# Block products for a third batch, denominators from added tiles, and plain float32 scores

## The chip, the cores and the metric

The kernel runs on one core of one Trainium2 chip. The metric is device time in microseconds (us) of one execution, as the median of several runs. TensorE multiplies matrices into PSUM; VectorE, ScalarE and GpSimd work on SBUF and (but for GpSimd) PSUM; SyncE only issues DMAs.

## What is computed

The reference is attention for 4 batches of 12 heads (448 positions, head size 64) with a tanh cap on the scores, followed by two matrix products with a squared ReLU between them:

```python
scores = scale * np.matmul(q, k.transpose(0, 1, 3, 2))
scores = cap * np.tanh(scores / cap)
attn = np.exp(scores - np.max(scores, axis=-1, keepdims=True))
attn = attn / (np.sum(attn, axis=-1, keepdims=True) + 1e-09)
attn_out = np.matmul(attn, v)
x = attn_out.transpose(0, 2, 1, 3).reshape(B * S, H * D)   # 1792 x 768
r = np.maximum(x @ w_in, 0.0)                               # w_in 768 x 2048
out = (s * (r * r) + b) @ w_out                             # w_out 2048 x 768
```

The two weight matrices arrive as float64 and are turned into float32 bit by bit on the chip.

## The kernel before

**Attention.** Two heads make a pair, so a batch has 6 pairs. `load` fetches a pair's keys and queries (`kq`) and values. It also splits `kq` into a rounded part and a remainder, both float32r, in the tile `kh`: one copy (`kq_hi`, L371 to L376) and one subtraction (`kq_lo`, L377). `scores` computes one chunk of 128 keys against all 448 queries. For each of the two heads it multiplies three times (high by high, high by low, low by high), so a chunk is six float32r matmuls on 64 rows (L396). The last 64 keys of two pairs share one chunk, the tail, which has always used the unsplit float32 `kq` (L404). ScalarE then takes tanh (L408) and exp (L412) of each chunk. `pv` multiplies the chunks with the values in float32, four 32-column tiles side by side (L460, label `value`), and sums the same chunks with columns of ones for the denominators (`total`, L468): two calls of four float32 matmuls for each pair. A list `ADDED` can send a batch another way: the three full chunks are first added elementwise into the tile `acc` (label `add`), and one call of four matmuls sums that tile and the tail. Before, `ADDED` is empty.

**Products.** Values go through the two products as pairs of float16 tiles, high and low, with three matmuls for each product. `m1` is the first product, in steps of 9 matmuls with 448 columns (L706 to L708). The second has two forms. `m2` (L942 to L944) multiplies all of `w_out`: 24 steps of 12 matmuls with 448 columns for a batch. `m2pair` (L854, label `m2p`) works with seven half-width block products instead of eight: 42 steps of 12 matmuls with 224 columns for a batch. That form wants more from the other engines: sums and differences of the squared values (`less`, L805), their split (`e_hi`, `e_lo`), and mixed weights `ws` made once by `mix(p)` for each of three pairs of output blocks (`mcopy`, `mfull`, `msums`, `m_hi`, `m_lo`, L745 to L782), saved to HBM (`savem`) and loaded again (`load2`). Batches in `FAST` take it; before, these are 2 and 3.

**Order.** The program's operations are recorded by `Plan` and issued by hand: `ORDER` lists every operation by number, with a letter where ScalarE, VectorE or GpSimd can each do it (a, d, p). Each engine runs its part of that list in order. `SLOTS` says how many buffers each pool has; for example `ps_v`, the PSUM tile of `value` and `total`, has one.

Of the kernel before, what the change touches and what calls it, by code (L numbers as in the profile page):

```python
# [21 lines left out]
class Plan:  # L22
# [87 lines left out]
FAST = (2, 3)  # L110
ADDED = ()
# [3 lines left out]
    "w": 7, "kq": 3, "vp": 3, "ph": 5, "pt": 2, "rd": 3, "pw": 3, "num": 9, "cmp": 3, "x": 6, "r": 4, "sq": 5, "cs": 2,  # L115
    "kh": 2, "acc": 2, "ps_s": 2, "ps_v": 1, "ps_m": 2,
}
ORDER = """
9 10d 11d 0 921 13 20 4 17 5 21 922 923 14d 853 15d 915 22 854 855 26 18 924d 909 50 916 3 925 917 910 918d 859
27 12 911 23 19 856d 912d 926d 51 33 24 28 47 74 919 25 29 53 920a 865 48 52 913 999 34 30 78 16 977 54 31 860 6  # L120
# [12 lines left out]
247 295 1051 323 269 951 249 199 272 270 945 175d 298 324 46 326 329 952p 1052d 138 250 1055 946p 248 1062 251
273d 8 350 1056 947 252 305 201 276 309 277 942a 200 953 351d 304 325 306 301 330 274 355a 1057 367 352d 202d
327 111 307 275 328 176 954a 1058p 364 308 310 203 368 948a 278 876 1020 204 1059 279 358 311a 1063 357 331 280
313 205 955 435 206 332 365 281 1060a 336 333 359 207a 209a 1053 1064p 282 1027 956 334 361 356d 391 1065 211d
1054a 210 362 312 957 208 212 958 337 335 392 1066a 283p 394 388 1067 363 1476 431 395 1068 253 353 360 366 213a
1069 217d 338d 432p 448 1070 1071d 1072 254 963d 374 255 315 1095 433d 370 369 959a 371 389 215a 372 218 216 960
393 1073a 1074 214 390 375 373 1021 1075a 449 434 1077 445 1494 907d 964 1028 961a 342 1477 905d 436a 314 1495
446 256d 1029 1096 437d 442 439 1030a 376a 1097 401 397 443 396 1478 903a 440 398 1022 1033 1 1496 341 908 1031  # L140
316 339 496 1076 1032a 1023 1034 317 441 377 1089 399 450 318 402 319 400 1035 962 1036d 906 1024d 1497 472 475
1025 497a 320 1524 1525 1037 904 1090 498d 1078 1083 1026a 321d 1079 1488 447 1091 1038a 1526 1039 1489 1040
1041 476 403a 444 513 455 1098p 473 340 503 451 1084 1080a 1490 378 1085 1042 1099 452 404 514 1043a 1100 1086a
1491 1092d 642 438 380 453 1093 1094 1479 454 456 343 379 1081 1082 381 1045a 504 469 382 1087 1088 344 1482
1480a 1483 1492a 477 1493p 1518 505 1044 1527 1528a 474 1484 1101d 1108 257 470 1046 1109 510 1110 1047a 561 471
1113a 1115a 383 384 407 385 507 1519 501d 345 386d 1529d 457a 506 459 1560 478 482 1117p 284 387 1102d 1123p
1116 1111d 346 347 1498a 1125a 1103d 511 508 1118 460 483 479 480 1520 1048 481 406 502d 534 537 1561 1199 562a
1121a 348p 1124 1530 1126 405 1187 535 1181 499 538 1481d 1200 515 484a 1201 565 1122 1531 1188 1112 1189 1119d
2 1120 408 1182 409 1183 1202a 1114 1104d 1184d 1193 1185 1203 1499d 1521 512 540 1194 1195 1196d 578 461 1190a
509 516 563d 520 458 1562 1197 517 518 1204 521 519 1522p 1532 566a 1191 1198 1523p 567p 711 1105p 1563 541 579  # L150
536 1500 1501 1502 1503 1192 1186 572 569 410 1212 1213 1214 1227a 1564a 1485 1554 1205d 1504p 412 1106 411 539
1229a 413d 1565p 1533 1107 1555 1534a 1512 322 1206p 1513 1556 414 349 1228 646 1470 522a 1535p 1223p 1225a
1486p 1514 1505d 415 1471 573 570 1472 1473 580 1207d 488 485 487 486 489 1230 523 1217d 524 525 416 526 574
1219a 1226 1474a 1215d 1487d 543 542 527 571 547 602 575 1224 1557 1506 1221p 417 1507 1220 1218 1515 1508 462
1222 1536 1475p 463 1509 1516d 1558d 1216 1517d 1208d 1510a 710 1291 1292 1548 1549 1550 1293 1285 1286 1537
1294p 576 219 1287 490 1288d 1295 1566 1538 1511d 1303 1551 1567 1542 1539 1231 1127 1570 1209p 643a 1543 1552d
1584 1289 1544 1545 1540p 1297 544 545 546 548 599 1290 1128 1541d 528 1304 424a 1305 1546a 1210 603 1306d 1309d
1307 644d 1559p 1298 1553p 1299 1568 1296 1300p 1301 1308 464 1302 1211 1316 600 1317 1547p 1569 1310d 601 465
1318 1598 1327d 418a 1329a 1330 1331a 1333a 1311d 1332 605 491 492 493 494p 1334 659 647d 1328 529 1323a 530
549a 428a 466 426d 1580 1319d 1581 429 1324 1232 660 1571a 577 1321p 531 1582 564 1325a 585 581 648d 582 1312d  # L160
419 1326 583 584 586 1239 1240 1241 430 1242a 1233 1320 1322 1243 653 1245 1234 1244 1246 553 1251 604 1235 606
650 1247 532d 1336 551 1236a 651 587a 1248d 552 654 1252 707 645 655 1253 1594 1583 1237 1254d 1255 1335 1238
1595 1249 1256 568 1250 1313p 1264 1585a 591 1257d 467d 607 1265 1596 1266 1314 1279a 550 1147 1258d 1597 1591
1280 683 1275d 656 1259d 1271a 608 1315 609 1281d 1277d 1282 652 1273a 612 1148 1149 1274 1269d 1135 772 1150a
657 1267p 590 589 588 610 613 708d 611 680 1151 1278 1276 1270 1136 1129 1272 1599d 592 684 420d 724 658 614a
618 616 554 662 1152 661 681 555 556 663 709d 666 1141 1586 593 1268 594 427 422a 1137 725 1130 1131 423 664
1138a 1142 1143 1144d 1139 1132a 667 665 776 686 557 1260d 718 1133 1145 595 1146 685 726 719 1284 649 615 1134
1153p 596 682 1587 687 1588 1140 495 688 712a 558 617 1589 1160 1261p 597p 1161 1337 1162 1154d 1590 668a 559d
# [52 lines left out]
def attention_moe_kernel(  # L221
# [14 lines left out]
    D = 64  # L236
# [839 lines left out]
```

## Time and profile before

| | us |
|---|---|
| median of 3 runs (636.55 to 637.71) | 637.59 |
| the profiled execution | 638.84 |
| its span on the core | 637.1 |
| TensorE busy | 619.6 (97%) |
| VectorE busy | 420.9 (66%) |
| ScalarE busy | 355.3 (56%) |
| GpSimd busy | 143.7 (23%) |

In the views, PE is TensorE, PEld its weight loads, DVE VectorE, ACT ScalarE, POOL GpSimd, SP SyncE, and L12 is line 12 of the kernel. A float32 matmul shows as two records, a float16 or float32r matmul as one. The end of a matmul is modelled and lies past the start of the next, so the distance between starts tells what a matmul costs.

### The profile page before, as it was taken

The numbers are of one execution on the slowest core, as the hardware profiler recorded it, in microseconds if no ns is written. First come the engines' busy times: TensorE is split into PE (matmuls) and PEld (weight loads), VectorE is DVE, ScalarE is ACT, GpSimd is POOL, SyncE is SP. The second block draws the span as 40 slices with busy tenths as digits, with TensorE's granted clock in tenths as the row PEclk, the third lists the DMA queues.
The fourth block names the chain that finished last, engine by engine and source line by source line (L and its number), as shares of the span: only waits on it lengthen the run. The fifth ranks groups of instructions, "written<-read, shape, count | busy, mean of one in ns | idle before, by whom it ended". The sixth has DMA issues, their size and how long they took to land.

```text
span 637.1 us, 11673 instructions
## 1 busy us (share of the span) xinstructions
PE 619.6 (97%) x4548; PEld 343.7 (54%) x4548; DVE 420.9 (66%) x898; ACT 355.3 (56%) x490; POOL 143.7 (23%) x180
## 2 busy tenths in 40 slices
PE   5998999999999999999999999999999999999997
PEld 2333334444445444545445555555558996556997
DVE  6999789997978989798374472427674342355312
ACT  6999989998784756675455352234463101354100
POOL 0101131113453201412040233002253000246000
PEclk9998989999999999999999999999999999999999
DMA  7884654643335373653452324425166751500763
GB/s 291 289 252 135 198 166 154 212 141 127 111 94 163 119 272 130 222 186 105 144 180 100 123 106 151 162 99 195 34 228 256 232 180 46 215 1 1 227 221 117
DMA packets 51318, 101.68 MB, mean 160 GB/s; under 512 B 15808, under 2 KB 28224, under 8 KB 51264
## 3 DMA queue, kind: packets, MB, share of 16 engines
q1 hardware_dynamic: 51264, 100.95, 47.3%
q8 instruction: 35, 0.57, 0.4%
q14 instruction: 19, 0.16, 0.1%
HBM read 82.58 MB, written 18.17 MB: 158 GB/s over the span
## 4 chain that ended last, share of the span: by engine, by line
PE 76%; DVE 11%; DMA 9%; SPq 2%; issue 1%; POOL 0%; ACT 0%; POOLq 0%; ACTq 0%
PE ps_m L854 9%; PE ps_v L460 7%; PE ps_s L854 6%; PE ps_s L707 6%; PE ps_s L708 6%; PE ps_s L706 6%; PE ps_m L706 5%; PE ps_m L707 5%; PE ps_m L708 5%; PE ps_m L942 4%; PE ps_m L943 4%; PE ps_m L944 4%; PE ps_s L396 4%; PE ps_v L468 4%; DMA bed<-in_w_out 3%; DMA zd<-bed 2%
## 5 line engine op out<-in xcount | busy, mean ns | idle before, releaser
L854 PEld LDWEIGHTS <-bed 128*128 128x128 f16 x1008 | 96.5, 98 | 0.9
L408 ACT ACTIVATE bed<-ps_s,arena 128x896 f32<-128x896 f32 x84 | 83.1, 1009 | 23.9 <-PE ps_v L460 9.4
L328 POOL TENSOR_TENSOR bed<-bed 128x224 f32<-128x224 f32 (+5 forms) x51 | 53.6, 1059 | 170.0 <-ACT bed L798 91.2
L327 DVE TENSOR_TENSOR bed<-bed 128x224 f32<-128x224 f32 (+5 forms) x95 | 66.7, 721 | 36.0 <-DMA bed<-zd 15.4
L460 PE MATMUL ps_v<-bed 128*32 128x448 f32 x768 | 85.7, 552 | 3.1 <-DMA bed<-in_v 2.4
L412 ACT ACTIVATE bed<-bed,par 128x896 f32<-128x896 f32 x84 | 85.2, 1044 | 0.2
L707 PE MATMUL ps_m<-bed,w 128*128 128x448 f16 x192 | 67.9, 353 | 0.0
L707 PE MATMUL ps_s<-bed,w 128*128 128x448 f16 x192 | 67.8, 353 | 0.0
L706 PE MATMUL ps_m<-bed,w 128*128 128x448 f16 x192 | 67.5, 352 | 0.3 <-DVE arena L661 0.3
L942 PE MATMUL ps_m<-gt,bed 128*128 128x448 f16 x192 | 67.7, 352 | 0.0
L944 PE MATMUL ps_m<-gt,bed 128*128 128x448 f16 x192 | 67.7, 352 | 0.0
L943 PE MATMUL ps_m<-gt,bed 128*128 128x448 f16 x192 | 67.7, 352 | 0.0
L706 PE MATMUL ps_s<-bed,w 128*128 128x448 f16 x192 | 67.4, 351 | 0.0
L708 PE MATMUL ps_m<-bed,w 128*128 128x448 f16 x192 | 67.2, 350 | 0.0
L708 PE MATMUL ps_s<-bed,w 128*128 128x448 f16 x192 | 67.2, 350 | 0.0
L396 PE MATMUL ps_s<-kh 64*128 64x448 f32 x432 | 58.6, 393 | 6.2 <-DVE kh L373 4.6
L706 PEld LDWEIGHTS <-w 128*128 128x128 f16 x384 | 36.8, 96 | 39.3 <-issue 4.7
L396 PEld LDWEIGHTS ps_s<-kh 64*128 64x128 f32 x432 | 37.9, 189 | 37.2 <-issue 9.3
L794 ACT ACTIVATE bed<-ps_s,arena 128x448 f32<-128x448 f32 x32 | 20.2, 631 | 66.3 <-PE ps_s L708 57.5
L708 PEld LDWEIGHTS <-w 128*128 128x128 f16 x384 | 37.8, 98 | 35.4
L707 PEld LDWEIGHTS <-w 128*128 128x128 f16 x384 | 37.0, 96 | 34.4 <-issue 0.6
L460 PEld LDWEIGHTS ps_v<-bed 128*32 128x32 f32 x768 | 22.7, 111 | 48.9 <-issue 41.9
(126 smaller groups left out, 966.9 us busy)
## 6 DMA issues: line engine op xcount, KB each, us to landing
bed<-w SPq DMA_DIRECT2D x36, 512.0 KB, 4.2
bed<-in_w_out SPq DMA_DIRECT2D x24, 512.0 KB, 4.1
bed<-ws SPq DMA_DIRECT2D x24, 512.0 KB, 4.9
bed<-in_kq SPq DMA_DIRECT2D x24, 448.0 KB, 4.7
bed<-in_w_in SPq DMA_DIRECT2D x18, 512.0 KB, 5.6
bed<-in_v SPq DMA_DIRECT2D x24, 256.0 KB, 4.2
w<-bed SPq DMA_DIRECT2D x12, 512.0 KB, 5.0
ws<-bed SPq DMA_DIRECT2D x12, 512.0 KB, 4.3
```

Of the source, the lines that this page charges most:

```text
L327: "DVE": lambda: nc.vector.tensor_tensor(dst(), a(), c(), op),
L396: nc.tensor.matmul(P[kp][:, h, 0:S], a[:, kz, 0, c * 128:(c + 1) * 128], a[:, qz, 1], start=i == 0, stop=i == 2,)
L408: ("tanh", bb, c2, c), lambda: nc.scalar.activation(P[ke], P[kp][:, :, 0:S], AF.Tanh, scale=tsc[:, 0:1]),
L412: ("exp", bb, c2, c), lambda: nc.scalar.activation(P[ke], P[ke], AF.Exp, scale=par[:, 0:1]), r=["par"], w=[ke],
L460: nc.tensor.matmul(P[kp][o, 0, 0:S], P[kv][:, c, o], prob(c, h), start=(c == 0), stop=(c == NC))
L706: nc.tensor.matmul(ps[:, 0:S], wh, x[:, 0], start=(c == 0), stop=False)
L707: nc.tensor.matmul(ps[:, 0:S], wh, x[:, 1], start=False, stop=False)
L708: nc.tensor.matmul(ps[:, 0:S], wl, x[:, 0], start=False, stop=(c == NP - 1))
L854: nc.tensor.matmul(at(), w(g, zw), b(g, zb), start=g == 0 and x == 0, stop=g == n - 1 and x == 2,)
L942: nc.tensor.matmul(ps[:, 0:S], wh, ghi[:, f], start=(f == 0), stop=False)
L943: nc.tensor.matmul(ps[:, 0:S], wh, glo[:, f], start=False, stop=False)
L944: nc.tensor.matmul(ps[:, 0:S], wl, ghi[:, f], start=False, stop=(f == NF - 1))
```

## The change

`FAST` becomes batches 1, 2 and 3, `ADDED` becomes batches 1, 2 and 3, and a new list `SPLIT` leaves the float32r split of keys and queries to batch 3. Batches 0 to 2 compute their full chunks as `plain`: one float32 matmul for each head from the unsplit `kq`. The pool `kh` shrinks from two tiles to one, `acc` has one tile, `w` grows to eight. The DMA of `cap` is issued from ScalarE's queue. `ORDER` is new throughout.

```diff
-FAST = (2, 3)
-ADDED = ()
+FAST = (1, 2, 3)
+ADDED = (1, 2, 3)
+SPLIT = (3,)
 SLOTS = {
-    "w": 7, ...
-    "kh": 2, "acc": 2, "ps_s": 2, "ps_v": 1, "ps_m": 2,
+    "w": 8, ...
+    "kh": 1, "acc": 1, "ps_s": 2, "ps_v": 1, "ps_m": 2,
...
     def load(bb, c2):
...
-        kx = buf(("kh", bb, c2), "kh")
...
+        if bb in SPLIT:
+            kx = buf(("kh", bb, c2), "kh")
...
+        def plain():
+            for h in range(2):
+                a = P[("kq", bb, c2)][h * D:(h + 1) * D]
+                nc.tensor.matmul(P[kp][:, h, 0:S], a[:, 0, c * 128:(c + 1) * 128], a[:, 1], start=True, stop=True)
...
+        if last:
+            pe(("tail", bb, c2, c), rest, r=pair, w=[kp])
+        elif bb in SPLIT:
+            pe(("score", bb, c2, c), mm, r=[(kx, 0), (kx, 1)], w=[kp])
+        else:
+            pe(("plain", bb, c2, c), plain, r=pair[0:1], w=[kp])
...
+        queue = nc.sync if i else nc.scalar
```

The operations that change in number, from the lists of both kernels:

| operation | before | now |
|---|---|---|
| `score` (6 float32r matmuls) | 72 | 18 |
| `plain` (2 float32 matmuls) | 0 | 54 |
| `total` (4 float32 matmuls) | 48 | 30 |
| `m2` steps / `m2p` steps | 48 / 84 | 24 / 126 |
| `kq_hi` on VectorE, ScalarE, GpSimd | 10, 12, 2 | 0, 6, 0 |
| `kq_lo` on VectorE, GpSimd | 23, 1 | 5, 1 |
| `add` on VectorE, GpSimd | 0, 0 | 34, 2 |
| `less` on VectorE, GpSimd | 37, 27 | 55, 41 |
| `e_lo` on VectorE, GpSimd | 9, 7 | 20, 4 |
| `plus` on VectorE | 48 | 72 |

The first instructions on VectorE, before (`kh` is the split tile, `par` and `arena` hold constants, L540 and L545 unpack float64 weights):

```order
L373 CAST kh_64<-bed 128x896
L327 TENSOR_TENSOR kh_64<-bed,kh_64 128x896
L975 RECIPROCAL arena<-par 128x1
L976 TENSOR_SCALAR arena<-arena 128x1
L540 TENSOR_SCALAR bed<-bed 128x512
L545 SCALAR_TENSOR_TENSOR bed<-bed 128x512
L373 CAST kh_65<-bed 128x896
```

and now:

```order
L991 RECIPROCAL arena<-par 128x1
L992 TENSOR_SCALAR arena<-arena 128x1
L556 TENSOR_SCALAR bed<-bed 128x512
L561 SCALAR_TENSOR_TENSOR bed<-bed 128x512
L325 TENSOR_SCALAR bed<-bed 128x512
L567 SCALAR_TENSOR_TENSOR bed<-bed 128x512
```

The casts and subtractions for the first scores are gone, and the unpacking of weights stands first.

TensorE around the denominators of a pair of batch 1, before (L460 `value`, L468 `total`, L396 `score`):

```order
L460 MATMUL ps_v_68<-bed 32x448 x4
L468 MATMUL ps_v_68<-bed,ones 32x448 x4
L460 MATMUL ps_v_68<-bed 32x448 x4
L396 MATMUL ps_s_66<-kh_65 128x448 x6
L460 MATMUL ps_v_68<-bed 32x448 x4
L468 MATMUL ps_v_68<-bed,ones 32x448
L468 MATMUL ps_v_68<-bed,half 32x448
```

and now (L476 `value`, L484 `total`, L409 `plain`):

```order
L476 MATMUL ps_v_67<-bed 32x448 x8
L409 MATMUL ps_s_65<-bed 128x448 x2
L409 MATMUL ps_s_66<-bed 128x448 x2
L476 MATMUL ps_v_67<-bed 32x448 x4
L484 MATMUL ps_v_67<-bed,ones 32x448
L484 MATMUL ps_v_67<-bed,half 32x448
```

The first of the two `total` calls is gone, and each score is two matmuls in place of six.

VectorE now, on the way into batch 1's second product (L772, L781 to L784 and the 128x8x128 rows are `mix(1)`; rows of 128x224 are `less`, of 128x672 `e_lo`, on `gt` `g_lo`; L901 adds a block product):

```order
L772 SCALAR_TENSOR_TENSOR bed<-bed,arena 128x1024 x2
L781 TENSOR_TENSOR bed<-bed 128x4x128
L782 TENSOR_TENSOR bed<-bed 128x4x128
L783 TENSOR_TENSOR bed<-bed 128x4x128
L784 TENSOR_TENSOR bed<-bed 128x4x128
L332 TENSOR_TENSOR bed<-bed 128x224
L332 TENSOR_TENSOR gt<-bed,gt 128x448
L332 TENSOR_TENSOR bed<-bed 128x224
L332 TENSOR_TENSOR bed<-bed 128x8x128 x2
```

Before, the two mixes of the first pair of blocks stood among plain steps of batch 1, and nothing of batch 1 read what they made.

## Rows read from the trace of the kernel before

**Rows 1.** The page: busy time, share of the span, instructions of an engine.

```profile
PE 619.6 (97%) x4548; PEld 343.7 (54%) x4548; DVE 420.9 (66%) x898; ACT 355.3 (56%) x490; POOL 143.7 (23%) x180
```

**Rows 2.** Windows: stretch, length, busy time (count) of PE, PEld, DVE, ACT, POOL, granted clock, DMA.

```profile
0.00:20.00 20.00, 13.62 (x92) 5.58 (x92) 13.64 (x28) 12.74 (x15) 1.34 (x11) 1.00 0.84 314
20.00:60.00 40.00, 36.21 (x363) 14.99 (x363) 38.90 (x90) 40.00 (x50) 5.24 (x10) 1.00 0.68 217
60.00:100.00 40.00, 37.83 (x329) 14.54 (x325) 34.43 (x91) 35.73 (x42) 8.44 (x13) 0.91 0.53 162
100.00:140.00 40.00, 40.00 (x349) 17.86 (x341) 38.02 (x90) 39.99 (x56) 7.48 (x9) 1.00 0.59 195
140.00:180.00 40.00, 39.30 (x280) 19.01 (x277) 34.51 (x75) 32.42 (x49) 16.40 (x14) 1.00 0.36 113
180.00:220.00 40.00, 40.00 (x247) 19.41 (x246) 33.27 (x78) 25.09 (x40) 15.52 (x20) 1.00 0.36 114
220.00:260.00 40.00, 39.31 (x297) 17.77 (x296) 33.57 (x78) 27.60 (x35) 2.77 (x6) 1.00 0.62 211
260.00:300.00 40.00, 39.54 (x282) 19.55 (x280) 36.62 (x84) 25.50 (x34) 14.51 (x20) 1.00 0.47 157
```

**Rows 3.** Waits of PE: waiter, releaser, us in total, times, longest.

```profile
PE ps_s L396 <- DVE kh L373: 4.6, 1, 4.6
PE ps_v L460 <- DMA bed<-in_v: 2.4, 2, 1.4
```

**Rows 4.** Timeline of PE from 99.6: start, duration, line, operands, count.

```profile
99.96 1.69 PE L460 MATMUL ps_v<-bed 128*32 128x448 f32 x16
101.58 1.48 PE L396 MATMUL ps_s<-kh 64*128 64x448 f32 x12
102.99 0.18 PE L362 MATMUL ps_m<-brief,ones 128*128 128x1 bf16 x1
...
106.47 0.35 PE L706 MATMUL ps_m<-bed,w 128*128 128x448 f16 x1
...
108.18 0.17 PE L362 MATMUL ps_m<-brief,ones 128*128 128x1 bf16 x1
108.28 0.98 PE L404 MATMUL ps_s<-bed 64*64 64x448 f32 x8
109.19 0.96 PE L468 MATMUL ps_v<-bed,ones 128*32 128x448 f32 x8
109.96 2.44 PE L460 MATMUL ps_v<-bed 128*32 128x448 f32 x24
```

**Rows 5.** Timeline of PE in a second product of each form.

```profile
392.06 0.35 PE L943 MATMUL ps_m<-gt,bed 128*128 128x448 f16 x1
...
394.33 0.35 PE L943 MATMUL ps_m<-gt,bed 128*128 128x448 f16 x1
...
601.40 1.31 PE L854 MATMUL ps_m<-gt,bed 128*128 128x224 f16 x12
602.55 1.31 PE L854 MATMUL ps_m<-bed 128*128 128x224 f16 x12
```

**Rows 6.** Groups of DVE by line and shape: busy us, mean ns, idle before.

```profile
L551 DVE SCALAR_TENSOR_TENSOR bed<-bed 128x512 int32<-128x512 int32 x42 | 32.0, 772 | 1.2 <-POOL bed L321 0.6 <-ACT bed L319 0.4
L327 DVE TENSOR_TENSOR kh<-bed,kh 128x896 fp32r<-128x896 f32 x23 | 25.0, 1087 | 0.1
L338 DVE SCALAR_TENSOR_TENSOR bed<-bed,arena 128x256 f16<-128x256 f32 x48 | 24.6, 531 | 3.5 <-ACT bed L319 2.9 <-POOL bed L321 0.6
L327 DVE TENSOR_TENSOR bed<-bed 128x224 f32<-128x224 f32 x37 | 19.9, 556 | 13.8 <-ACT bed L798 7.5 <-POOL bed L328 6.0
L327 DVE TENSOR_TENSOR bed<-bed 128x672 f16<-128x672 f32 x9 | 8.6, 954 | 1.3 <-ACT bed L319 1.2
```

**Rows 7.** The page's DMA issues: size, median us from issue to landing.

```profile
bed<-ws SPq DMA_DIRECT2D x24, 512.0 KB, 4.9
ws<-bed SPq DMA_DIRECT2D x12, 512.0 KB, 4.3
```

More of the change, by code (lines that the diff above doesn't have):

```diff
@@ L114 @@
 SLOTS = {
[L115 to L116 removed]
+    "w": 8, "kq": 3, "vp": 3, "ph": 5, "pt": 2, "rd": 3, "pw": 3, "num": 9, "cmp": 3, "x": 6, "r": 4, "sq": 5, "cs": 2,
+    "kh": 1, "acc": 1, "ps_s": 2, "ps_v": 1, "ps_m": 2,
 }
 ORDER = """
[L119 to L120 removed]
@@ new lines @@
+856 917d 959 107 104 105 861d 976 90 38 86 87 131 862 915a 91 62 108 106 109 863 88 89 916 960 39 92a 135 136
+144 145 60 40 869 988 989 990d 957 113 961 208 864 918 857d 858 94 146 962d 865 963 977 991 61 93 112 96 95 978d
+141 866d 117 870 142 114 165 41d 867 137 97 132 138 115 116 871 98 118 59 875 166 143 63 168 139 931 119d 64
+872p 876 167 171 147 140 873 877 914 99 878d 148 981 120 121 65 879 982 932 169 149 964a 170 100 101 983 933
+859d 151 874a 152 134 212 868a 880a 881 172 123 122 150 958a 979 213 173 965 102p 966 984d 934p 124 215 967 218
@@ new lines @@
+326 267 1065 323 204 371 417 1056 1058 205a 202 206 299 1009 422 1004 269d 426 1506 427 941a 300 425 942 945d
+885a 1536 1537 1538 1507 324 997a 301 377 1005 1006a 357a 1452 337 946 382d 1010 1453 1016 1011 448 428 378 1071
+1059 1017 383d 2 327 358 361 360 1508 1012a 1018a 1454 1007 418 303 302 379 384 889d 1072 1013 419 1060 1019
+1020a 328 1014a 1008a 380 359 381 998 890 1073 1458 1509 887a 1021 476 304d 1074a 449 1459 1077 414 329 1455
+385a 450 362 1022 1023 433d 451 452 454 1456a 888 434d 387 330 429 1066 388 435 430 431 1078 1061 363 1024 455
@@ new lines @@
+516 1478 1172a 1184a 441 492 468 1496 547 493 1097a 1185 394 465 1086d 548 1087d 494 618 495 1166a 442 395p 1175
+1186 498 1500 1088 1511d 1501 466 574 1099p 1173 1100 1167 1474a 518 1176 1089 524d 1479 443 1177 543 542 499a
+500 1178d 619a 519 525d 1179 1502 1475p 520 575 503 521 1093a 1480a 522 1180 444 1168 1481p 270 445 544 501
+1095a 1497 1174 469 523 526 549 580 1482 1194 502 446d 470 576 550 1195 620d 1094 1483 1196 504 581 545 471 396
+1098 1187p 1188p 552 551 1484 1205a 527d 242 1464 1465 531 530 368 528 505 1209d 629 559d 1096 1503 553 560d
@@ new lines @@
+693 1545 1227 1235 1217 1218a 665 690a 1222 1236d 1237 1535d 1546p 1238 1223 670d 1523d 1224a 702 703 666 571
+667 1550 1564 671d 694 407 1225 1219 1214 599 1228 1239d 1229 1552 755 1547d 1220 704 1230a 598 1226 1565 650
+1231 691d 447 1551 651 572p 404a 1240p 1567a 1232 1246 1247 1248 668 672 1317 752 1259p 405 1261d 1260 695 1251a
+1252 1249a 1250 1257a 698 408a 669 1255a 692 1241d 727 724 1576 709p 673a 1253d 1263d 600d 701 728 1254 1256
+1129 1577 675 652 730 1117 725 769 676 729 674 753a 1242d 705 1264 1258 710d 711 731 726 706 707 411 1111 708
@@ L404, in rest @@
                     nc.tensor.matmul(P[kp][x * D:(x + 1) * D, h, 0:S], a[:, 0, c * 128:S], a[:, 1], start=True, stop=True)
-        pe(("tail" if last else "score", bb, c2, c), rest if last else mm, r=pair if last else [(kx, 0), (kx, 1)], w=[kp])
+        if last:
[4 more added lines that the diff above has]
+            pe(("plain", bb, c2, c), plain, r=pair[0:1], w=[kp])
         act(
@@ L992, in attention_moe_kernel @@
     for i, a in enumerate((cap, s, b)):
-        dma(("par", i), lambda i=i, a=a: nc.sync.dma_start(par[:, i:i + 1], a.to_broadcast([128, 1])), w=[("par", i)])
+        queue = nc.sync if i else nc.scalar
+        dma(
+            ("par", i), lambda i=i, a=a, queue=queue: queue.dma_start(par[:, i:i + 1], a.to_broadcast([128, 1])),
+            w=[("par", i)],
+        )
     gps(("units", -1), units, w=["one"])
```

186 lines of the change are left out of this document (86 added, 100 removed), and 8 rows, old and new, of the table ORDER.

## The prediction

> **What bounds the kernel now.** I read the page's first part, then the windows, then the waits and the timeline of TensorE. TensorE is busy 619.6 of 637.1 us [rows 1]. The windows show where it is not: 6.4 us are missing in the first 20, 3.8 from 20 to 60, 2.2 from 60 to 100, and from there under 1 us in any 40 us [rows 2]. The missing time belongs to the beginning, where VectorE is 97% and ScalarE 100% busy from 20 to 60. The longest single wait is the very first score's, 4.6 us for the first split of keys [rows 3]; the clock share of 0.91 from 60 to 100 is the other loss there [rows 2].
>
> Busy time hides small gaps, since ends are modelled. So I price TensorE by distances between starts. Two `value` chunks with the switch to another tile form take 101.58 - 99.96 = 1.62 us, so 0.75 a chunk and about 0.11 a switch; a `total` call is the same, 109.96 - 109.19 = 0.77; two scores take 1.41, 0.705 each; a tail takes 0.91 with a switch, 0.80 without; an `m1` step of nine 1.71 [rows 4]; an `m2` step of twelve 2.27, an `m2p` step 1.15 [rows 5]. Over the whole list: 128 x 1.71 + 48 x 2.27 + 84 x 1.15 + 144 x 0.75 + 72 x 0.705 + 12 x 0.80 = 593 us, some 106 switches at 0.1 make 10.6, and the small products for norms and biases 4.9, together 608. The span is 29 longer: 4.6 to the first matmul, about 3 for the last output, and some 21 of waiting, nearly all before 100 us. I call **lead** the time of a TensorE instruction less the TensorE work ahead of it. By the trace it grows to 21 us by 95 and stays near 23.5 from 190 on. So TensorE's own work and this lead are all that counts.
>
> **TensorE's work.** *Denominators:* batches 1 to 3 drop one `total` call for each of 18 pairs, 18 x 0.75 = 13.5 us less. *Second product of batch 1:* 24 steps of 2.27 (54.5) become 42 of 1.15 (48.3), 6.2 less. *Plain scores:* 54 of them. No row shows this form, so bounds: a plain score is two float32 matmuls, four records in two rounds, as in a `value` chunk, which streams the same 448 columns: 0.75 from below. The tail is the nearer relative (same operands, same 64 rows, weights of 64 columns instead of 128) and gives 0.80, or 0.91 if each carries a switch. I take 0.78, near the tail, since a score's 128-column loads cost it only about 0.05 for each round over 0.187 of streaming [rows 4]. That is 0.075 more than a split score, 54 x 0.075 = 4.1 more; ends +2.4 and +11. Fewer matmuls here is not less time.
>
> The Trainium skill (FP8 and Floating Point Precision, TensorE Precision Notes) counts four passes for true float32, against three for the split: it speaks against this edit, and the chunk of 0.75, four times the 0.19 of an `m1` matmul, agrees [rows 4]. The skill's Perfetto Trace Analysis (Engine Utilization) instead has float32 in its low and high form at half the output rate; by that a plain score would be 0.37 and the sum 22 us lower, and the chunk row disagrees.
>
> *Switches* rise from 106 to 111: 0.5 more. TensorE's sum is -13.5 - 6.2 + 4.1 + 0.5 = **-15.1 us**, 608 to 593.
>
> **The other engines.** The split disappears for three batches: VectorE loses 18 subtractions at 1.09 us and 10 casts, ScalarE 6 copies. This work stood in front of the first scores; the first score now needs only its load, and ScalarE's first tanh waits for `cap`, whose DMA leaves about half a microsecond sooner on ScalarE's queue and no longer stands in SyncE's. In return VectorE gets 34 additions over 896 columns (nearest row 1.09 each), 18 `less` at 0.56, 11 `e_lo` at 0.95 [rows 6] and 24 `plus`. All kinds together, VectorE's durations rise by some 41 us. Durations add up to 470 in the trace of before against 420.9 busy [rows 1], since neighbours overlap, so 0.895 of that: +36 us. ScalarE gains about 9.
>
> VectorE's place matters more than its sum. `mix` must now be ready for batch 1, some 100 us of TensorE work sooner than for batch 2. The tightest point is the second mixed pair of blocks: TensorE's third product there waits for the load of `ws`, that waits for its save, and that for the last `m_lo` of its first half. Ahead of that `m_lo`, by the new order and the rows of before, stand on VectorE: weight unpacking 101 us (rows like L551), `w_out` 73 (L338 and others), attention with 33 additions 72, `w_in` 42, `g_lo`, `less` and `e_lo` 41, `mix` 37, the rest 26: 392, times 0.895 = 350 us. TensorE's work ahead of its product is 358. Up to the same `m_lo`, VectorE's work before was 0.895 x 341 = 305 and nobody waited for it.
>
> The lead that this forces: VectorE starts at about 5.5 us, works 350 at some share s, then save and load take 4.3 + 4.9 [rows 7]. In stretches where much waits in its queue s was 0.97 (20 to 60), 0.95 (100 to 140), 0.92 (260 to 300); over 20 to 300 it was 249.3 of 280, 0.89, but much of that idle time was TensorE's doing [rows 2]. I take 0.955, between the two stretches in which both engines were full. Then the load lands at 5.5 + 366.5 + 9.2 = 381.2, and the lead is 381.2 - 358.4 = 22.8, against 23.5 before: **-0.7 us**. What the beginning gains (VectorE's queue ahead of a score was up to 13 us longer than TensorE's before, at most 4 now) is thus spent again by 380 us. After that point VectorE has 20 us and more in hand, and the end of the program is unchanged.
>
> Edits at nothing: the smaller `kh` and `acc` pools (the order already holds to them; if one tile is too few it shows as VectorE waiting for TensorE), and 18 more loads of 512 or 256 KB for batch 1: the same form's loads moved during batches 2 and 3 without a wait.
>
> **Sum.** From the profiled execution, 638.84 - 15.1 - 0.7 = 623.0. That execution lies 1.25 above the median of the runs, so **622** for a median.
>
> **The rivals.**
>
> *A, the forecast:* s from 0.935 to 0.97 gives leads from 29 to 17; with the ends of the plain score 615 to 630. Chance 0.63.
>
> *B, VectorE becomes the bound.* Place: the same `m_lo` and the additions on the way to it, each of which a `total`, and with the single `ps_v` the next pair's values, waits for. If s stays at the 0.89 of 20 to 300, the load lands at 408, the lead is 49.5, and the time 622 + 27 = 649. It decides at a lead of 38.6, s = 0.916: below that the kernel is slower than before. For it: VectorE reached 0.86 from 60 to 100 while TensorE waited [rows 2]. Against it: the queue that delayed TensorE there is now shorter. Chance 0.12 for slower, and 0.08 for the ground between A and the point of deciding, 630 to 638.
>
> *C, the beginning's gain stays.* With s at 0.97 or more and GpSimd taking its part, the lead falls to 14 to 16: 614, down to 611 with the cheapest plain score. For it: 20 to 60 did 0.97 with all engines full. Chance 0.12.
>
> *D, a plain score's two heads do not run side by side:* 54 x 0.75 = 40 more on TensorE, which then stands ahead of VectorE again: about 655. Against it: a split score's pair of heads does run side by side, six matmuls in 0.705 [rows 4]. Chance 0.02.
>
> *E, a plain score streams at half rate,* not a quarter: its 448 columns in two times the 0.19 of an `m1` matmul [rows 4], 0.38. That takes 54 x 0.40 = 22 us off TensorE's work, to 600 if TensorE alone sets the time; but all of it lies ahead of the tight point, where VectorE would keep most of it. Chance 0.03.
>
> **How the numbers follow.** A is likeliest: 622. The range takes in A, C and the ground between and leaves out most of B, D and E: 611 to 636. About 0.2% (1.3 us) is what a measurement can tell from no change. Faster: A, C, E and most of the ground between, 0.83; same, the rest of that ground, 0.03; slower, B and D, 0.14.
>
> **What would show it.** Right: plain scores 0.75 to 0.80 apart; `m2p` steps of batch 1 at 1.15; total matmul work near 593; TensorE's first matmul near 4 us; less idle TensorE before 100 us, and then some waits of TensorE between 100 and 380 for VectorE (`add`, `mix`) or for the loads of `ws`; VectorE's busy time near 457, its share up to 370 us about 0.95. Wrong: a plain score above 0.9; no waits after 100 us at all (C); or a lead above 30 at batch 1's `m2p` (B).

## The result, and the profile after

The changed kernel took 619.81 us (median of 4 runs, 618.26 to 620.61) where the kernel before, on the same chip, took 637.65 (636.55 to 638.56): a ratio of 0.972, 95% interval 0.969 to 0.975. The forecast was faster, 622, with a range of 611 to 636. The profiled execution took 619.09 us, with a span of 616.9, against 638.84 and 637.1 before. Experiments ran on several chips; each is compared by its ratio to the kernel before, timed on the same chip. The changed kernel, measured a second time beside the experiments, had 0.966 (0.964 to 0.969), so about 0.969 is its place on that scale, and 0.01 is 6.4 us.

The page of the changed kernel (answers to [rows 1]):

```profile
PE 603.0 (98%) x4512; PEld 347.6 (56%) x4512; DVE 450.7 (73%) x957; ACT 363.5 (59%) x509; POOL 158.1 (26%) x177
```

Its windows (columns as in [rows 2]: stretch, length, PE, PEld, DVE, ACT, POOL, granted clock, DMA):

```profile
0.00:20.00 20.00, 13.41 (x92) 4.37 (x92) 10.45 (x22) 13.17 (x15) 4.21 (x12) 1.00 0.85 327
20.00:60.00 40.00, 38.97 (x337) 12.50 (x338) 37.45 (x98) 39.16 (x47) 10.13 (x14) 1.00 0.63 208
60.00:100.00 40.00, 38.68 (x329) 12.84 (x325) 37.97 (x98) 38.34 (x46) 8.59 (x14) 1.00 0.64 194
100.00:140.00 40.00, 40.00 (x295) 16.07 (x291) 37.89 (x79) 39.21 (x55) 14.91 (x11) 1.00 0.58 177
140.00:180.00 40.00, 39.64 (x272) 16.16 (x264) 39.48 (x81) 37.34 (x55) 14.62 (x15) 1.00 0.34 100
260.00:300.00 40.00, 40.00 (x263) 19.49 (x262) 37.77 (x91) 20.82 (x31) 13.88 (x14) 1.00 0.47 151
340.00:380.00 40.00, 40.00 (x338) 29.36 (x335) 34.54 (x56) 25.07 (x39) 8.71 (x9) 1.00 0.63 224
```

Against [rows 2] TensorE gains 2.8 us of work from 20 to 60 and 0.9 from 60 to 100, and the clock share there is 1.00 in place of 0.91. VectorE is now 36 to 39.5 of 40 full all the way to 340, where before it had 33 to 35 from 140 to 260. ScalarE is full to 140. The waits of TensorE are short but for the first (waiter, releaser, us in total, times, longest; compare [rows 3]):

```profile
PE ps_s L409 <- DMA bed<-in_kq: 6.1, 1, 6.1
PE ps_m L367 <- DVE brief L684: 1.1, 2, 0.8
PE ps_v L476 <- DVE bed L505: 1.0, 2, 0.6
PE ps_v L476 <- DMA bed<-in_v: 0.4, 1, 0.4
```

**Where the 20.2 us of span went.** I laid every TensorE instruction of both traces against the operation it belongs to, and took the distance to the next start where nothing waits as that operation's price; what goes beyond it is waiting (time lost at half clock included). This gives:

| us | before | after | |
|---|---|---|---|
| TensorE's work | 605.9 | 591.7 | -14.2 |
| first matmul | 4.6 | 6.1 | +1.5 |
| waiting to 100 us | 17.5 | 8.9 | -8.6 |
| waiting after 100 us | 4.4 | 5.9 | +1.5 |
| after the last matmul | 3.3 | 3.0 | -0.3 |

By kind the work changed by -13.6 (`total`, 37.3 to 23.7), -6.3 (`m2` and `m2p`, 204.6 to 198.3) and +5.8 (`score` and `plain`, 53.1 to 58.9), each with its switches. The last matmul step itself, 1.3 us in both kernels, is in no row. Every plain score is counted here at 0.85, but 15 of the 54 take 0.95 (13 that stand alone between other tile forms, two behind a wait). With these 1.5 us as work and not as waiting, the work fell by 12.7 and all the rest by some 7.4. So 13 to 14 us are work that is gone, and 9 to 10 are waiting in the first 100 us that is gone; 3 of these come back, half as a later start and half behind 100 us.

### The profile page after: what moved, and what is told of

Its sections match the earlier page's. It is cut to its first block, busy times and chain, and to the rows that moved or that the text cites. A ratio compares the mean times of both kernels' runs of the same rounds, so it can differ in the third digit from the quotient of the medians.

```text
span 616.9 us, 11696 instructions
## 1 busy us (share of the span) xinstructions
PE 603.0 (98%) x4512; PEld 347.6 (56%) x4512; DVE 450.7 (73%) x957; ACT 363.5 (59%) x509; POOL 158.1 (26%) x177
## 4 chain that ended last, share of the span: by engine, by line
PE 70%; DVE 14%; ACT 6%; DMA 5%; issue 2%; SPq 1%; POOL 1%; POOLq 0%; ACTq 0%
PE ps_m L870 13%; PE ps_s L870 10%; PE ps_s L723 9%; PE ps_s L722 9%; PE ps_s L724 9%; PE ps_v L476 4%; DMA bed<-in_w_in 3%; PE ps_m L958 3%; DVE bed L332 3%; PE ps_m L960 2%; PE ps_m L959 2%; ACT bed L424 2%; PE ps_s L402 2%; DVE bed L567 2%; ACT bed L428 2%
## 5 line engine op out<-in xcount | busy, mean ns | idle before, releaser
L870 PEld LDWEIGHTS <-bed 128*128 128x128 f16 x1512 | 144.7, 98 | 3.9 <-issue 1.5
L332 DVE TENSOR_TENSOR bed<-bed 128x224 f32<-128x224 f32 (+6 forms) x161 | 119.8, 758 | 36.0 <-ACT bed L814 18.4
L723 PE MATMUL ps_s<-bed,w 128*128 128x448 f16 x288 | 101.8, 353 | 0.0
L333 POOL TENSOR_TENSOR bed<-bed 128x224 f32<-128x224 f32 (+6 forms) x61 | 65.0, 1072 | 142.4 <-ACT bed L814 36.1
L722 PE MATMUL ps_s<-bed,w 128*128 128x448 f16 x288 | 101.1, 351 | 0.0
L724 PE MATMUL ps_s<-bed,w 128*128 128x448 f16 x288 | 100.9, 350 | 0.0
L476 PE MATMUL ps_v<-bed 128*32 128x448 f32 x768 | 81.7, 543 | 1.3 <-DVE bed L505 1.0
L409 PE MATMUL ps_s<-bed 64*128 64x448 f32 x216 | 51.9, 583 | 6.8 <-DMA bed<-in_kq 6.1
L476 PEld LDWEIGHTS ps_v<-bed 128*32 128x32 f32 x768 | 21.8, 109 | 48.5 <-issue 38.3
L901 DVE SCALAR_TENSOR_TENSOR bed<-ps_m,arena,bed 128x224 f32<-128x224 f32 x45 | 19.3, 447 | 38.2 <-PE ps_m L870 38.0
L870 PE MATMUL ps_s<-gt,bed 128*128 128x224 f16 x432 | 45.3, 259 | 0.0
L870 PE MATMUL ps_m<-gt,bed 128*128 128x224 f16 x432 | 45.3, 259 | 0.0
L870 PE MATMUL ps_m<-bed 128*128 128x224 f16 x432 | 45.0, 259 | 0.0
L343 DVE SCALAR_TENSOR_TENSOR bed<-bed,arena 128x256 f16<-128x256 f32 (+1 forms) x72 | 40.8, 589 | 0.6 <-POOL bed L326 0.3
```

Of the source, the lines that this page charges most:

```text
L332: "DVE": lambda: nc.vector.tensor_tensor(dst(), a(), c(), op),
L333: "POOL": lambda: nc.gpsimd.tensor_tensor(dst(), a(), c(), op),
L343: lambda: nc.vector.scalar_tensor_tensor(lo(), src(), sc, hi(), ALU.mult, ALU.subtract),
L409: nc.tensor.matmul(P[kp][:, h, 0:S], a[:, 0, c * 128:(c + 1) * 128], a[:, 1], start=True, stop=True)
L476: nc.tensor.matmul(P[kp][o, 0, 0:S], P[kv][:, c, o], prob(c, h), start=(c == 0), stop=(c == NC))
L722: nc.tensor.matmul(ps[:, 0:S], wh, x[:, 0], start=(c == 0), stop=False)
```

## The experiments

**1. The second product of batch 1 alone undone.** Batch 1 takes the full form again; some ten other operations of the order stand elsewhere.

```diff
-        for d in range(ND // 2 if j in FAST else ND):
-            (m2pair if j in FAST else m2)(j, d)
+        for d in range(ND // 2 if j in FAST and j != 1 else ND):
+            (m2pair if j in FAST and j != 1 else m2)(j, d)
```

> The changed kernel with the full second product for batch 1 (24 steps of twelve 448-column matmuls in place of 42 of 224 columns; no sums, differences and their splits for that batch, the mixed weights at the same places in the order). TensorE 6.2 us more. Theory (VectorE had slack enough): 626.0. Rival (VectorE's work for the block products made TensorE wait): 620 to 622.

Measured: ratio 0.977 (0.974 to 0.980), 625.35 us. TensorE's work rises from 591.7 to 597.8, its waiting stays (15.0 against 14.8). By the spans of the profiled executions this is 6.6 us (623.5 against 616.9), by the ratio some 5: the block products bring their 6 us, and VectorE's extra work for them costs nothing here.

**2. The additions undone.** `ADDED` empty; the first `total` of each pair stands where its first `add` stood or a little behind, in 11 of the 18 pairs ahead of all `value` calls of the pair.

```diff
-ADDED = (1, 2, 3)
+ADDED = ()
```

> The changed kernel without the additions: batches 1 to 3 sum their chunks by two calls of four matmuls again. TensorE gets 18 x 0.75 = 13.5 us more, VectorE loses 34 x 1.04 = 35 us. Theory (VectorE was not what TensorE waited for): 619.8 + 13.5 = 633.3. Rival (VectorE sets the lead between 100 and 380): the lead falls by about 5, so 628.

Measured: ratio 0.998 (0.997 to 1.000): nearly the whole gain of the change is gone, more than either expectation had. TensorE's work is 606.9, 15.2 more, of which the 18 calls with their switches are 14.8. And waiting does not fall with VectorE's 37 us of additions, it rises, from 14.8 to 20.1. TensorE's new wait (same view as above; here L476 is `total` and L496 ScalarE's copy of `ps_v`):

```profile
PE ps_v L476 <- ACT bed L496: 3.5, 5, 1.1
```

Without the additions a pair's `total` calls hold the single `ps_v` for four matmuls longer, and the first instruction of the next pair, a `total`, waits five times until ScalarE has copied it out. VectorE has room in this kernel, 28.1 of 40 us busy from 60 to 100, and it is of no use. So the additions pay twice: work off TensorE, and a wait that is not there. That this wait comes from the longer hold of `ps_v`, and not from the place that this order gives to the first `total`, was not tested.

**3. Plain scores alone**, in the kernel before, for all four batches, in its own order without the split's operations. The pool `kq` has five tiles, since the unsplit keys are now held until the scores.

```diff
-        pe(("score", bb, c2, c), mm, r=[(kx, 0), (kx, 1)], w=[kp])
+        pe(("plain", bb, c2, c), plain, r=pair[0:1], w=[kp])
```

> The kernel before with plain scores alone, in all four batches (no split of keys and queries at all; five buffers for keys in place of three; the order is otherwise the one of before). A plain score took 0.85 us in the changed kernel, a split one 0.705 or 0.80 with the switch behind it: 72 x about 0.1 = 7 more TensorE work. Theory (in the kernel before the split in VectorE's queue made TensorE wait at the beginning): the lead at 100 us falls from 21.6 to about 15, so 638 in all, the same as before within 3. Rival (weights, loads or ScalarE set the beginning): lead unchanged, 645.

Measured: ratio 1.001 (0.999 to 1.003), no difference. TensorE's work rises by 8.1 us to 614.1, that is 0.113 for each of 72 scores; its waiting falls by 6.0, from 21.9 to 15.9, and the first matmul comes 0.6 sooner. In the windows of this kernel VectorE has become the emptier engine of the beginning, and TensorE is busy where it was not in [rows 2]:

```profile
20.00:60.00 40.00, 38.53 (x343) 12.46 (x344) 32.66 (x86) 38.16 (x47) 2.85 (x10) 1.00 0.70 218
```

This is what the theory said: the split in VectorE's queue held TensorE up in the beginning, and taking it out buys those 6 us at a price of 8 on TensorE. Two things are mixed in: 3.4 of the 6 us are half clock (see below), which this trace has nowhere, and the five key tiles were not tried alone. The plain scores are no gain by themselves. Their use is the room on VectorE, which the additions then fill (compare 37.45 in this stretch of the changed kernel). The additions without the plain scores were not run.

**4. More work on VectorE in three places, and on ScalarE in one.** The question: how near to its bound is the changed kernel, and where? In each, some instructions are issued twice into the same tile, with the order unchanged. TensorE's lead is read at one operation of batch 1, a `value` that the changed kernel starts at 91.7 us with a lead of 14.5 by the forecast's prices; the expectations call it the lead at 99 us. The first kernel doubles `g_lo` of batch 1 (15 on VectorE, about 10 us between 285 and 356):

```diff
-                [("gl", f)],
+                [("gl", f)], 2 if j == 1 else 1,
```

> The changed kernel with g_lo of batch 1 run twice where VectorE does it (some 14 times 0.68 = 10 us more VectorE work between 285 and 356 us, same result). Theory (the mixed weights of the second pair come only 1 to 2 us before TensorE wants them, so VectorE is next in line there): TensorE then waits on the load of the mixed weights or on VectorE, lead 5 to 9 us longer, 625 to 629. Rival (VectorE has slack): 620 to 621.

Measured: ratio 0.977 (0.974 to 0.980), 626.1 us, 7.4 more than the changed kernel on the same chip. TensorE's lead is much as in the changed kernel up to 300 us (21.4 against 20.3) and then goes to 28.5, mostly in two places: 3.8 us at 336, with 1.7 of half clock behind them, and 1.2 at 367. The first, in the waits of TensorE over the whole program and of ScalarE from 320 to 345:

```profile
PE ps_s L719 <- ACT bed L807: 3.9, 2, 3.6
```

```profile
ACT bed L317 <- DVE bed L326: 4.9, 1, 4.9
```

ScalarE stands at an `e_hi` whose differences VectorE has not made, and behind it in ScalarE's queue stands the emptying of a PSUM tile (L807) that TensorE's first product needs. So VectorE's lateness reaches TensorE through another engine's queue, before it reaches the mixes.

The second doubles the first `add` of each pair (16 on VectorE, 17.5 us between 65 and 355):

```diff
-            binary(("add", bb, c2, 1), ..., [kh[0], kh[1]], [ka])
+            binary(("add", bb, c2, 1), ..., [kh[0], kh[1]], [ka], 2)
```

> The changed kernel with the first addition of every pair of batches 1 to 3 run twice (18 x 1.05 = 19 us more VectorE work between 65 and 355 us, same result). Theory (VectorE is near its bound through 375 us): lead 12 to 19 us longer, 632 to 639. Rival (VectorE has slack, the lead comes from elsewhere): under 3 us longer, up to 623.

Measured: ratio 0.986 (0.983 to 0.988), 631.05 us, 12.3 more. The lead grows step by step: 19.6 at that `value`, 25.2 at 180, 28.4 at 248, 33.8 at 357, and then no further.

The third doubles the sign step of unpacking `w_in` (24 on VectorE, 16.8 us, in the changed kernel all before 120 us):

```diff
+            for _ in range(2 if label[0] == "i" else 1):
                 nc.vector.scalar_tensor_tensor(lo(), hi(), SIGN, lo(), ALU.bitwise_and, ALU.bitwise_or)
```

> The changed kernel with one step of the unpacking of w_in (the sign, 24 instructions of 0.70 us on VectorE, all within the first 120 us) computed twice: 16.8 us more VectorE work. Theory V (VectorE bounds the beginning): TensorE's lead at 99 us rises from 15 to 25 or more, and the time by 11 to 15 us. Theory S (ScalarE bounds the beginning, VectorE only the mixes of batch 1 near 370 us): the lead at 99 us rises by 5 us at most, TensorE's new waits stand mostly after 100 us, and the time rises by 9 to 13 us, because VectorE has only 2 to 6 us in hand there. Rival: VectorE has 17 us in hand over the first 370 us; then the time rises by under 2 us.

Measured: ratio 0.989 (0.986 to 0.992), about 13 us more than the changed kernel. The lead at that `value` is 26.5, 12 more, of which 1.7 are half clock: VectorE bounds the beginning. TensorE's longest new waits (columns as above) name VectorE:

```profile
PE ps_m L602 <- DVE bed L592: 3.6, 2, 2.4
PE ps_v L469 <- DVE bed L498: 3.3, 2, 2.7
```

The fourth doubles the tanh of the first chunk of each pair in batches 0 and 1 (12 on ScalarE, 12 us, before 110 us):

```diff
+            for _ in range(2 if bb < 2 and c == 0 else 1):
                 nc.scalar.activation(P[ke], P[kp][:, :, 0:S], AF.Tanh, scale=tsc[:, 0:1])
```

> The changed kernel with the tanh of the first chunk of every pair of batches 0 and 1 computed twice: 12 more ScalarE instructions of 1.01 us, 12 us in all, spread over the first 110 us. Nothing else is edited. Theory S (ScalarE bounds the beginning: it is 39.2 and 38.3 us busy of 40 from 20 to 60 and 60 to 100): TensorE's lead at 99 us rises from 15 to about 24 to 27, and the time by 8 to 12 us, since the work behind has only 2 to 6 us to give. Theory V (VectorE bounds it, 37.5 and 38.0 of 40; ScalarE merely follows): the lead at 99 us stays within 3 us of 15 and the time rises by under 3 us.

Measured: ratio 0.984 (0.981 to 0.987), some 9.4 us more. The lead at that `value` is 23.9, 9.4 more, and ScalarE bounds the beginning too. The two verdicts do not exclude each other, as the windows from 20 to 60 of the one with more on ScalarE (first) and of the one with more on VectorE (second) show:

```profile
20.00:60.00 40.00, 37.62 (x330) 11.95 (x326) 32.89 (x80) 39.80 (x47) 6.70 (x8) 1.00 0.57 180
```

```profile
20.00:60.00 40.00, 32.60 (x266) 10.44 (x262) 39.03 (x88) 32.45 (x38) 7.33 (x10) 0.96 0.54 170
```

With 4 us more on ScalarE or 7 on VectorE in this stretch, that engine is full and the other falls back to 32.5 to 33. In the changed kernel they stand at 39.16 and 37.45: the order has them balanced, and there neither has anything in hand. All four together: 10 to 17.5 us more on one engine cost 0.7 to 0.8 of themselves, wherever before 360 us they stand. The other way round it does not hold: what experiments 1 and 2 take off VectorE shortens no wait. That fits an order that stands just at the bound.

**5. The first 10 us.** Three kernels with the loads or the first scores in another order. The first moves the second pair's keys behind a piece of `w_in`:

```diff
-load(0,0) par load(0,1) loadw(i,2,0)
+load(0,0) par loadw(i,2,0) load(0,1)
```

> The changed kernel with one move: the second load of keys is issued behind the first load of weights, as in the kernel before, not right behind the first load of keys. Theory (the two key loads share the DMA engines and land together at 6.1 us): the first score starts at about 4.6 us instead of 6.1, and the lead gained is kept: 618.3 against 619.8. Rival (ScalarE, VectorE or the weights set the beginning anyway): first score sooner, time 619.8.

Measured: ratio 0.969 (0.966 to 0.971), as the changed kernel; the first matmul starts at 6.25 and not earlier. That two key loads share the way was the wrong idea. The second puts the load of `cap` back on SyncE's queue:

```diff
-        queue = nc.sync if i else nc.scalar
+        queue = nc.sync
```

> The changed kernel with the DMA of the cap back on SyncE's queue, second behind the first load of keys, as before. Theory (the cap's 144 packets of 4 bytes on a second queue run between the packets of the first key load and slow it, which is why moving the second key load alone left the first score at 6.3): first score at about 4.0 us, first tanh about 1.5 us sooner, 1 to 2 us less in all. Rival (ScalarE's and VectorE's work sets the beginning): first score at 4.0, time unchanged within 0.5.

Measured: ratio 0.966 (0.964 to 0.969), no change, although the beginning looks otherwise. The timeline of the changed kernel up to 10 us, all engines (start, duration, engine, line, operands; idle before and its end):

```profile
0.71 0.40 ACTq L1011 DMA_DIRECT2D par<-in_cap  x1
0.72 0.86 SPq L374 DMA_DIRECT2D bed<-in_kq  x2
...
6.11 1.87 PE L409 MATMUL ps_s<-bed 64*128 64x448 f32 x4 [6.11 <-DMA bed<-in_kq]
6.26 0.20 ACT L1016 ACTIVATE arena<-par 128x1 f32<-128x1 f32 x1 [3.83 <-DMA par<-in_cap]
...
7.91 1.77 PE L415 MATMUL ps_s<-bed 64*64 64x448 f32 x8
8.03 1.01 ACT L424 ACTIVATE bed<-ps_s,arena 128x896 f32<-128x896 f32 x1 [1.56 <-PE ps_s L409]
...
8.71 0.43 DVE L556 TENSOR_SCALAR bed<-bed 128x512 int32<-128x512 int32 x1 [2.09 <-DMA bed<-in_w_in]
```

and with `cap` on SyncE's queue:

```profile
0.72 0.39 SPq L367 DMA_DIRECT2D bed<-in_kq  x1
1.17 0.42 SPq L1004 DMA_DIRECT2D par<-in_cap  x1
...
3.83 1.87 PE L402 MATMUL ps_s<-bed 64*128 64x448 f32 x4 [3.83 <-DMA bed<-in_kq]
...
6.33 0.20 ACT L1009 ACTIVATE arena<-par 128x1 f32<-128x1 f32 x1 [4.33 <-DMA par<-in_cap]
...
6.78 1.01 ACT L417 ACTIVATE bed<-ps_s,arena 128x896 f32<-128x896 f32 x1 [0.25 <-DVE arena L985]
...
8.48 1.76 PE L408 MATMUL ps_s<-bed 64*64 64x448 f32 x4 [1.09 <-DMA bed<-in_kq]
...
9.75 0.43 DVE L549 TENSOR_SCALAR bed<-bed 128x512 int32<-128x512 int32 x1 [3.07 <-DMA bed<-in_w_in]
```

The first keys land 2.3 us sooner, the second pair's keys hold up the tail, and VectorE's first weights come 1 us later. `cap` itself is there at 6.26 on ScalarE's queue and at 6.33 on SyncE's, so its move gains nothing, and with the keys early the first tanh (6.78) waits for what is made of `cap`. The third kernel also moves that tail behind the first three chunks:

```diff
-plain(0,0,0) tail(0,0,3) plain(0,0,1) plain(0,0,2)
+plain(0,0,0) plain(0,0,1) plain(0,0,2) tail(0,0,3)
```

> The changed kernel with two edits: the load of cap back on SyncE's queue, and the first tail, which needs the second pair's keys, with its tanh moved behind the first pair's three plain chunks. With cap's load alone moved, the first key load landed at 3.8 us instead of 6.1, but the tail then waited 3.6 us for the second key load. Theory: the first four scores now run from 3.8 us without a long wait, ScalarE's first tanh starts near 6.8 instead of 8.0, and since ScalarE bounds the beginning TensorE's lead at 99 us falls by about 1 us and the time by 0.5 to 1.5 us. Rival: the beginning is set by VectorE or by the loads of weights, and what the first scores gain is given back by 60 us: within 0.5 us of the changed kernel.

Measured: ratio 0.970 (0.967 to 0.973), no gain; the rival was right. The first score starts at 4.0, VectorE's first piece of weights at 9.5, and at that `value` the lead is 16.5, 2 more than in the changed kernel. What the first scores gain is given back by then. That it is lost to VectorE's later start is likely but not shown: with the second key load moved VectorE started a microsecond sooner (7.6), and the time was the same.

**6. GpSimd takes ten operations of the first 100 us**, since it is the only engine with room there: five squares from ScalarE, five normalisations from VectorE.

```diff
-sq(4,2) sq(5,2) sq(5,0) sq(3,0) sq(7,2) on ScalarE; norm(0,0) norm(0,1) norm(0,3) norm(0,5) norm(1,0) on VectorE
+all ten on GpSimd
```

> The changed kernel with ten operations of the first 100 us given to GpSimd, which is busy only 10 of 40 us there: five squares of weights (0.71 us on ScalarE each, so 3.5 us less for ScalarE) and five normalisations (0.64 us on VectorE each, 3.2 us less for VectorE). The places in the order stay. Theory (ScalarE and VectorE together bound the beginning, and each of their microseconds there costs about 0.75 of one in the time): TensorE's lead at 99 us falls by 2 to 3 us and the time by 1.5 to 3 us, to a ratio near 0.966 on a scale on which the changed kernel has 0.969. Rival: GpSimd takes two to three times as long for each and stands between DMAs of the reciprocals, so that what waits for it gives the gain back: within 1 us of the changed kernel, or slower.

Measured: ratio 0.976 (0.972 to 0.979), 624.08 us, some 4 us slower than the changed kernel: the rival, and more than it said. One place shows both of its causes, and a third. ScalarE's waits from 40 to 110 us:

```profile
ACT bed L497 <- POOL bed L326: 3.8, 2, 2.3
ACT bed L591 <- POOL bed L441: 2.5, 1, 2.5
```

In the changed kernel ScalarE waits for GpSimd in this stretch nowhere. GpSimd works its queue in order, waits there 29 us for the DMAs of the denominators and their reciprocals, and ScalarE's queue waits for it. And VectorE and GpSimd near 62 us (timelines of the one and the other):

```profile
61.08 3.08 DVE L336 SCALAR_TENSOR_TENSOR w<-bed,arena,w 128x512 f16<-128x512 f32 x2
64.08 1.52 DVE L560 SCALAR_TENSOR_TENSOR bed<-bed 128x512 int32<-128x512 int32 x1
```

```profile
62.13 2.93 POOL L593 TENSOR_TENSOR bed<-bed 128x512 bf16<-128x512 f32 x2
```

An L560 takes 0.70 us when GpSimd stands still, and 1.52 here. The Trainium skill (SBUF — State Buffer, SBUF: two separate sides) says that VectorE, when it reads two inputs from SBUF, and GpSimd exclude each other from a shared port for a whole instruction; the two rows agree with it. And TensorE, which waits 1.9 us for the square that ScalarE makes late at 65.7 (its timeline), has the granted clock at 0.50 from 68.0 to 71.4 (window), some 1.6 of the 4 us:

```profile
66.40 0.40 PE L602 MATMUL ps_m<-ones,bed 128*128 128x1 bf16 x10 [1.91 <-ACT bed L591]
```

```profile
68.00:71.40 3.40, 3.11 (x13) 1.05 (x14) 3.16 (x15) 2.93 (x4) 0.00 (x0) 0.50 0.21 69
```

None of these versions beats the changed kernel.

## Why the prediction was right, step by step

**TensorE's work: -15.1 forecast, -14.2 measured.** The `total` calls (-13.5 forecast, -13.6 measured) and batch 1's second product (-6.2, -6.3) came as priced. The plain score was mis-sized: 4.1 and half a microsecond of switches were forecast, 5.8 measured at 0.85 for each, and 7.3 with the lone ones at 0.95; TensorE's work fell by 12.7 then. TensorE's timeline of the changed kernel (answers to [rows 4]):

```profile
125.85 1.77 PE L409 MATMUL ps_s<-bed 64*128 64x448 f32 x8
127.55 0.96 PE L476 MATMUL ps_v<-bed 128*32 128x448 f32 x8
...
129.08 2.44 PE L476 MATMUL ps_v<-bed 128*32 128x448 f32 x24
131.45 1.77 PE L409 MATMUL ps_s<-bed 64*128 64x448 f32 x8
133.16 0.36 PE L722 MATMUL ps_m<-bed,w 128*128 128x448 f16 x1
```

Two scores take 127.55 - 125.85 = 1.70, so 0.85 each, whether a `value` or an `m1` follows (133.16 - 131.45 = 1.71). A score that stands alone between other forms takes 0.95 (96.53 - 95.58):

```profile
95.58 1.02 PE L409 MATMUL ps_s<-bed 64*128 64x448 f32 x4
96.53 0.45 PE L609 MATMUL ps_m<-ones,bed 128*128 128x1 bf16 x12
```

The forecast took 0.78, between a chunk's 0.75 and the tail's 0.80 to 0.91. The wide range that it kept, up to 0.91, was the right one. Rivals D (two heads one after the other, 1.5) and E (half rate, 0.38) are out by these rows. An `m2p` step of batch 1 is 1.15: the two that start at 381.34 below end where the next starts, at 383.64.

**VectorE's path to the mix: on time, by luck.** The forecast had the last `m_lo` at 372.0, the load of `ws` landing at 381.2. VectorE, SyncE and TensorE in the changed kernel:

```profile
371.36 1.22 DVE L332 TENSOR_TENSOR bed<-bed 128x1024 f16<-128x1024 f32 x1
```

```profile
372.61 1.81 SPq L797 DMA_DIRECT2D ws<-bed  x2
376.89 2.04 SPq L853 DMA_DIRECT2D bed<-ws  x3
```

```profile
381.34 2.46 PE L870 MATMUL ps_m<-bed 128*128 128x224 f16 x24
383.64 0.55 PE L870 MATMUL ps_s<-gt,bed 128*128 128x224 f16 x4
```

The `m_lo` ends at 372.58, the save is issued at once, the load when the save has landed (4.3 us later), and the product that reads it is the second of the pair that starts at 381.34, at 382.49. The load took 3.5 us, not 4.9, and landed at 380.4, so the product does not wait; 2.1 us are in hand. VectorE's busy time was 450.7 (457 forecast), and from 20 to 340 us it was 302.8 of 320 busy, 0.946. Over the forecast's own stretch, from 5.5 to the end of the `m_lo`, it was this (windows, columns as above):

```profile
5.50:372.58 367.08, 361.67 (x2562) 162.07 (x2563) 340.89 (x738) 293.24 (x392) 104.28 (x106) 1.00 0.57 187
```

That is 341 us of work where the forecast had 350, at a share of 0.929 where it took 0.955: two errors of some 10 us that cancel. With 350 us at 0.929 the same sum gives a load at 391 and a lead of 33. (And at the lower end of rival A, s = 0.935, the forecast's figures give 30.6 and not 29.)

**The lead: -0.7 forecast, -5.6 measured. This is the step that failed.** "What the beginning gains is thus spent again by 380 us" is not what happened. Its mechanism, a lead that the mix of batch 1 forces, did not act at all. First matmul and waiting together are 26.5 before and 20.9 after. Three numbers in it were off. The product that needs the load stands 3.5 us further back in TensorE's list than the forecast had it: with the forecast's own prices 361.9 us of work lie ahead of it, not 358.4, so that the load's 381.2 forces a lead of 19.3, not 22.8. The kernel before had, by the same prices, 25.2 at that place and not the 23.5 read off for "190 and on". And TensorE's own waits up to 300 us already made the lead 20.3, more than the mix forces. So the tight point was found, its time too, but it was just not binding, and the gain of the beginning stayed, as rival C has it. C's time, 611 to 614, took a lead of 14 to 16, which was reached (14.5 at 91.7 us) but not held: up to 250 us some 5 us more were waited, never more than 1.7 in 10 us. Those are the waits that the forecast wanted to see between 100 and 380; none of them is for `ws`.

**Rival B was near.** The share up to the `m_lo`, 0.929, is below the range of A and not far above the 0.916 from which B has the kernel slower; that it cost nothing is owed to the smaller work. The experiments with more work on VectorE show that VectorE is the next bound everywhere before 360 us: 10 us there cost 7.4 and 17.5 cost 12.3, so by the same rate some 25 us would take the whole gain of 18 (an estimate).

**The first matmul near 4 us: wrong, and without a price.** The load of `cap` on ScalarE's queue delays the first keys to 6.1. The forecast counted the half microsecond by which `cap` leaves sooner, and not what its load does to the next one. With `cap` back on the other queue the first score starts at 3.83, and the time is the same. In all ten traces with `cap` on ScalarE's queue the first score starts at 6.1 to 6.3; in the three with plain scores and `cap` on SyncE's, at 3.8 to 4.0.

**The half clock.** The forecast named it as a loss and gave it no term. In the trace of before it stands behind short waits of TensorE, as here (windows, columns as in [rows 2]):

```profile
80.00:81.00 1.00, 0.34 (x4) 0.22 (x8) 1.00 (x4) 1.00 (x2) 0.00 (x0) 0.86 0.68 180
81.00:84.00 3.00, 3.00 (x20) 1.06 (x16) 3.00 (x5) 0.71 (x2) 0.16 (x1) 0.50 1.01 362
```

0.50 is 1.2 GHz. There were two such stretches of 3.4 us before 100 us, 3.4 us of TensorE's time, and none in the changed kernel (1.00 in every window above). So 3.4 of the 8.6 us of waiting that went were not waits but their echo. The runs agree: all eight of the changed kernel have a mean granted clock of 1.000, those of the kernel before, timed beside the experiments, 0.992 to 1.000.

The forecast's sum was 623.0 for the profiled execution, which was 619.1: -15.1 - 0.7 against -14.2 - 5.6 - 0.3. The price of the plain score was 1.2 too low (2.7 with the lone ones), the gain of the beginning nearly 5 too small, and both stayed inside the range. What carried the forecast is the first term, some three quarters of the gain; the second came out well only in its sign.

## What to carry to other kernels

Where two engines are balanced to 95%, ask of every operation on the way to the tight point what it costs at 0.7 to 0.8 of its length, and count TensorE's work ahead of the waiting instruction to that very instruction: 3.5 us miscounted there are most of what the forecast of the lead missed. An edit that is worth nothing alone (plain scores, 1.001) can be what pays for another one (additions, some 19 us with it), by the room it leaves on the engine that the other fills; that the pair needs each other is argued here, since the additions were not run without the plain scores. And work that is moved to an idle engine brings that engine's queue with it: ten operations on GpSimd cost 4 us where 2 were hoped for.

## What the runs showed of the hardware

- A float32 score with 128 weight columns on 64 rows takes 0.85 us for two heads side by side when another one stands next to it and 0.95 alone between other tile forms, against 0.705 for six float32r matmuls and 0.80 for the tail with 64 weight columns.
- The 0.5 KB load of `cap` on ScalarE's queue, issued with the first key load of 448 KB on SyncE's, brings those keys at 6.1 us instead of 3.8. The Trainium skill (DMA: Bandwidth & Descriptors, Issuing engines are not separate DMA queues) says that loads from several issuing engines run on the same 16 engines and interleave, which agrees.
- Stretches of 3.4 us at the granted clock 0.50 stood behind waits of TensorE of 1.4 us (the kernel before, at 80.7), 1.9 (ten operations on GpSimd), 2.7 (sign doubled) and 3.6 (`g_lo` doubled), and one in the kernel before, at 60.2, behind three waits of 0.3 to 1.0 in 2 us. But waits of 1.8, 1.8 and 1.9 in three other kernels (plain scores alone, `add` doubled, tail later) had none behind them, so the length of one wait doesn't tell. In the kernel with `g_lo` doubled (windows):

```profile
336.00:340.00 4.00, 0.41 (x3) 0.10 (x1) 3.93 (x8) 3.41 (x5) 1.12 (x1) 0.99 0.00 0
340.00:343.00 3.00, 3.00 (x9) 1.18 (x8) 3.00 (x3) 3.00 (x6) 0.90 (x1) 0.50 0.45 182
```

  The waiting there cost 1.7 us more behind it.
- Beside two GpSimd operations on 128x512 elements, VectorE's two-input operations took 1.5 us each instead of 0.7 to 0.8.
